# Block attention and FFN on one core: the FFN's first products join the attention's ring of PSUM banks, and the order of a far pair's steps changes

## The chip, the cores and the metric

The kernel runs on one core of a Trainium2 chip. The metric is the device time of one execution in microseconds (us); the time of a version is the median of several runs. The engines are TensorE (matrix products; PE in the profile, its weight loads PEld), VectorE (DVE), ScalarE (ACT), GpSimd (POOL) and SyncE (SP), which issues the DMAs. Products land in PSUM, which has 8 banks of 128 x 512 fp32; VectorE and ScalarE read them from there.

## The reference

Shapes: 8 batches, 8 heads, 576 tokens, head size 64; the FFN takes 4608 tokens of width 512 to 2048 and back.

```python
scores = (1.0 / np.sqrt(D)) * np.matmul(q, k.transpose(0, 1, 3, 2))
mask = block_i >= block_j              # blocks of 64 tokens
scores = np.where(mask, scores, -1000000000.0)
attn = np.exp(scores - np.max(scores, axis=-1, keepdims=True))
attn = attn / (np.sum(attn, axis=-1, keepdims=True) + 1e-09)
x = np.matmul(attn, v).transpose(0, 2, 1, 3).reshape(B * S, H * D)
h = x @ w_in
g = np.where(h >= 1, h, np.where(h <= -1, 0.0, (h + 1) ** 2 / 4.0))
out = g @ w_out
```

## The kernel before, in words

Every fp32 operand is held as a high and a low part, and each product is a sum of products of parts, so TensorE has much to do: 6280 products in all.

The attention works on 32 pairs of heads (4 per batch). A pair's work is cut into 8 steps (`attention_steps`, L663), each ended by a `yield`. From step START = 36 on (the fifth step of pair 4) the main loop at the end puts one step of the FFN behind each attention step: by turns `ffn_in` (L763: 12 products of 512 columns into one bank, `ph`, for 512 tokens and 128 of the 2048 columns) and `ffn_out` (L790: 12 products of 512 columns into the four output banks `po`). 66 FFN steps remain when the attention is over. The scheduler of the tile layer fixes the order on each engine when the program is built; it may move an instruction ahead of others, but not past what it depends on.

Pairs of batches 0 and 1 are "near" (and "plain": probabilities kept whole), those of batches 2 to 7 are "far": `self.far = b >= FAR`, FAR = 2. A pair's attention consists of

- scores: for the two heads j and three groups of query tiles g, `scores(j, g)` (L494), and `scores_last` for the last 64 tokens. TensorE makes the scores (L482, L485), VectorE finds the negated maximum (L505), ScalarE the exponential and its sum (L509), VectorE divides (L491, L492, L515), and a DMA copies the probabilities to a buffer `prr` of the type that TensorE turns (`as_float32r`, L230);
- turnings: `turn(j, g)` (L556) and `turn_last` (L572): TensorE transposes probabilities into a bank `ps_t` (L552), ScalarE writes the high part (L545), VectorE the low part (L547). The corner of the last block, a 128 x 64 piece, has a bank of its own in `turn_last`;
- attn*v: `attn_v_first` (the first 256 queries of both heads in one bank) and `attn_v(0)`, `attn_v(1)` (the other 320), products at L591 into `ps_av`; `add_halves` (L608) has ScalarE copy one half (L613) and VectorE add the other (L614). `xtmp`, where the copy goes, has one buffer;
- for the next pair, q and k turned: `turned_raw(j)` (L397) for each head and `turned_last` (L437) for the last blocks, into `ps_qk`; `parted` (L384) takes them out of the bank in turns of ScalarE and VectorE (L388, L389, L394, L395), `turned_last` with two more reads by VectorE (L446).

Every bank `ps_s`, `ps_t`, `ps_av`, `ps_qk` comes from `work_bank` (L80): before the FFN begins by turns from `ps_o`, the four output banks, and from `ps_w`; later from `ps_w` alone, a ring. A new tile of the ring takes the bank of the oldest one, so TensorE waits until the oldest tile's last reader is done. Before the change the ring `ps_w` has three banks, and `ph` a bank of its own (`ps_h`):

```python
ps_w = ctx.enter_context(tc.tile_pool(name="ps_w", bufs=3, space=bass.MemoryType.PSUM))
ps_h = ctx.enter_context(tc.tile_pool(name="ps_h", bufs=1, space=bass.MemoryType.PSUM))
ps_o = ctx.enter_context(tc.tile_pool(name="ps_o", bufs=NTT, space=bass.MemoryType.PSUM))
```

The last reader of `ph` is the maximum at L783, behind ScalarE's L779 and VectorE's L780.

## Time and profile before

| | us |
|---|---|
| median of 3 runs (lowest, highest) | 1269.29 (1268.47, 1269.56) |
| the profiled execution, its own time | 1269.69 |
| its span, first to last instruction | 1267.9 |
| TensorE busy in the span | 1200.1 |
| VectorE, ScalarE, GpSimd busy | 887.0, 703.2, 394.6 |
| mean granted TensorE clock, share of full | 0.981 |

The busy time of an engine counts overlapping instructions once. A row of the timeline gives the start, the time from start to end, and in brackets how long the engine had been idle and what ended that. Products are pipelined: one starts before the one ahead has ended, so the step from start to start is the price of a product, not its duration. Names of lines (L482) are those of the kernel before unless said otherwise; the change shifts lines below L515, so that L547 stands at L560 in it, L552 at L565, L591 at L608, L770 at L799, L794 at L823, L799 at L828.

### The profile page before, as it was taken

The page shows a single profiled execution, that of the slowest core. Times are in us where ns is not written, and L with a number is a line of the kernel's source. Part 1 is how long each engine was busy: PE and PEld are TensorE (multiplying, and loading weights), DVE is VectorE, ACT ScalarE, POOL GpSimd, SP SyncE. Part 2 cuts the span into 40 slices and gives each one's busy share as a digit, 9 for nine tenths or more (in the row PEclk, how much of TensorE's full clock was granted, in tenths as well). Part 3 has the DMA queues.
Part 4 walks back from the last instruction along what each step waited for, and adds up shares of the span by engine and source line. Part 5 has one row for each costly group of instructions (what it writes and reads, how often), then busy time and mean ns, then how long its engine had stood idle before and what let it go on. Part 6 is the DMA issues. An engine that isn't in the chain of part 4 may idle for free.

```text
span 1267.9 us, 20253 instructions
## 1 busy us (share of the span) xinstructions
PE 1200.1 (95%) x6280; PEld 998.8 (79%) x6280; DVE 887.0 (70%) x2188; ACT 703.2 (55%) x1827; POOL 394.6 (31%) x430
## 2 busy tenths in 40 slices
PE   5888889899999999999999999999999999999998
PEld 4666667678888888888888888888888888888886
DVE  8898877758777777777777777787777777322222
ACT  5787656646566655665656655566556555222222
POOL 3555655522222222222222222222222222222222
PEclk9888988999999999999999999999999999999999
DMA  5566666667888655555554655465556433422432
GB/s 158 167 176 215 203 228 197 217 198 237 260 273 266 215 162 158 154 175 163 156 162 145 187 157 152 138 189 153 160 154 190 137 128 118 132 87 98 133 100 100
DMA packets 185259, 215.43 MB, mean 170 GB/s; under 512 B 113840, under 2 KB 132272, under 8 KB 184384
## 3 DMA queue, kind: packets, MB, share of 16 engines
q1 hardware_dynamic: 185152, 214.14, 54.9%
q8 instruction: 50, 0.82, 0.3%
q14 instruction: 57, 0.47, 0.1%
HBM read 134.74 MB, written 31.98 MB: 131 GB/s over the span
## 4 chain that ended last, share of the span: by engine, by line
PE 69%; DVE 16%; ACT 6%; issue 5%; DMA 1%; POOL 1%; SPq 1%; ACTq 0%; POOLq 0%; DVEq 0%
PE ph L770 29%; PE po L794 15%; PE po L799 7%; PE ps_av L591 7%; PE ps_s L482 4%; ACT pr L509 3%; PE ps_s L485 3%; DVE t L780 2%; PE ps_t L552 2%; DVE t L783 2%; ACT t L779 2%; DVE pb L547 2%; DVE nm L505 2%; DVE sm L491 1%; DVE pr L515 1%
## 5 line engine op out<-in xcount | busy, mean ns | idle before, releaser
L785 POOL TENSOR_TENSOR gl<-t,gh 128x512 fp32r<-128x512 f32 x144 | 187.5, 1302 | 510.2 <-ACT gh L784 333.2
L794 PE MATMUL po<-wo,gh 128*128 128x512 f32 x1152 | 296.1, 397 | 0.5 <-DMA wo<-wo_split 0.3
L794 PEld LDWEIGHTS po<-wo,gh 128*128 128x128 f32 x1152 | 212.5, 189 | 44.5 <-DMA wo<-wo_split 0.7
L770 PE MATMUL ph<-xh,wih 128*128 128x512 f32 x576 | 232.9, 404 | 1.6 <-DVE t L783 1.6
L770 PE MATMUL ph<-xh,wil 128*128 128x512 f32 x576 | 228.8, 397 | 0.0
L770 PE MATMUL ph<-xl,wih 128*128 128x512 f32 x576 | 227.8, 396 | 0.5 <-DVE xl L627 0.5
L780 DVE SCALAR_TENSOR_TENSOR t<-t 128x512 f32<-128x512 f32 x144 | 101.5, 705 | 168.0 <-ACT t L779 165.2
L779 ACT ACTIVATE t<-ph 128x512 f32<-128x512 f32 x144 | 85.9, 597 | 173.8 <-PE ph L770 173.8
L509 ACT ACTIVATE pr<-ps_s,nm 128x128 f32<-128x128 f32 (+3 forms) x256 | 134.1, 527 | 60.5 <-DVE nm L505 58.4
L784 ACT CAST gh<-t 128x512 fp32r<-128x512 f32 x144 | 89.5, 621 | 120.3 <-DVE t L783 120.0
L799 PE MATMUL po<-wo,gl 128*128 128x512 f32 x576 | 155.6, 392 | 0.0
L482 PE MATMUL ps_s<-ka,qa 68*128 68x288 f32 (+4 forms) x384 | 135.3, 367 | 15.0 <-ACT pr L509 5.4
L379 POOL TENSOR_TENSOR vsr<-vn,vsr 128x256 fp32r<-128x256 f32 (+1 forms) x96 | 55.2, 576 | 246.2 <-ACT vsr L378 244.6
L770 PEld LDWEIGHTS ph<-xh,wil 128*128 128x128 f32 x576 | 109.5, 190 | 23.8
L770 PEld LDWEIGHTS ph<-xh,wih 128*128 128x128 f32 x576 | 109.8, 191 | 21.7 <-DVE t L783 2.3
L799 PEld LDWEIGHTS po<-wo,gl 128*128 128x128 f32 x576 | 108.7, 189 | 23.1
L505 DVE TENSOR_REDUCE nm<-ps_s 128x1 f32<-128x128 f32 (+3 forms) x256 | 118.8, 482 | 10.4 <-PE ps_s L485 9.4
L770 PEld LDWEIGHTS ph<-xl,wih 128*128 128x128 f32 x576 | 109.7, 190 | 20.5 <-DVE xl L627 0.9
L485 PE MATMUL ps_s<-kb,qb 128*128 128x288 f32 (+4 forms) x384 | 121.1, 322 | 0.0
L515 DVE TENSOR_SCALAR pr<-pr,sm 128x128 f32<-128x128 f32 (+3 forms) x256 | 107.3, 440 | 5.4
L783 DVE TENSOR_TENSOR t<-ph,t 128x512 f32<-128x512 f32 x144 | 98.7, 686 | 2.2
L491 DVE TENSOR_SCALAR sm<-sm 128x1 f32<-128x1 f32 (+1 forms) x224 | 52.0, 232 | 68.3 <-ACT pr L509 65.7
(111 smaller groups left out, 1871.4 us busy)
## 6 DMA issues: line engine op xcount, KB each, us to landing
wo<-wo_split SPq DMA_DIRECT2D x144, 512.0 KB, 3.5
prr<-pr SPq DMA_DIRECT2D x96, 192.0 KB, 2.5
prr<-pr SPq DMA_DIRECT2D x72, 256.0 KB, 2.8
out_dram<-ob SPq DMA_DIRECT2D x36, 256.0 KB, 2.9
bits<-in_moe_w_in_dram SPq DMA_DIRECT2D x32, 256.0 KB, 3.5
bits<-in_moe_w_out_dram SPq DMA_DIRECT2D x32, 256.0 KB, 3.0
wo_split<-ws SPq DMA_DIRECT2D x16, 512.0 KB, 2.9
qa<-qb SPq DMA_DIRECT2D x63, 128.0 KB, 2.4
```

The source lines that it names most:

```text
L482: nc.tensor.matmul(ps, qa[:KA, j, c0 : c0 + P], ka[:KA, j, k0 : k0 + n], start=first, stop=False)
L485: nc.tensor.matmul(ps, qb[:, j, c0 : c0 + P], kb[:, j, k0 : k0 + n], start=False, stop=last)
L505: nc.vector.tensor_reduce(out=nm[:, i : i + 1], in_=ps[:, cs], axis=AX.X, op=ALU.max, negate=True)
L509: nc.scalar.activation(pr[:, cs], ps[:, cs], AF.Exp, bias=nm[:, i : i + 1], scale=1.0, accum_out=sm[:, i : i + 1],)
L515: nc.vector.tensor_scalar_mul(pr[:, cs], pr[:, cs], sm[:, i : i + 1])
L770: nc.tensor.matmul(ph, w[:, cc, fs], x[:, cc, xs], start=(cc == 0 and i == 0), stop=(cc == NCC - 1 and i == 2),)
L779: nc.scalar.activation(t_, ph, AF.Relu, bias=0.5, scale=0.5)
L780: nc.vector.scalar_tensor_tensor(out=t_, in0=t_, scalar=1.0, in1=t_, op0=ALU.min, op1=ALU.mult)
L783: nc.vector.tensor_tensor(out=t_, in0=ph, in1=t_, op=ALU.max)
L785: nc.gpsimd.tensor_tensor(out=gl, in0=t_, in1=gh.bitcast(F32), op=ALU.subtract)
L794: nc.tensor.matmul(po[tt], gh[:, ts_], wo[:, w, :], start=(fc == 0 and w == 0), stop=False)
L799: nc.tensor.matmul(po[tt], gl[:, ts_], wo[:, 0, :], start=False, stop=fc == NFC - 1)
```

## The change

The pool `ps_h` goes, `ps_w` gets a fourth bank, and `ffn_in` takes its bank from `work_bank`. For far pairs: scores come first in every step, and the copy DMA of the probabilities is issued at the end of the step (`move`); attn*v's three parts stand in steps 1, 2 and 3 of the next pair (they stood in step 8 and in steps 1 and 3); the last block's corner is turned in the bank of `turn(1, 0)`; q and k of the next pair's second head are turned in step 7 and its last blocks in step 8 (they stood in step 8 and in the next pair's step 2). `attn_v_first` takes `xtmp` once for both heads. No product, reduction or DMA is added or taken away.

```diff
-    ps_w = ctx.enter_context(tc.tile_pool(name="ps_w", bufs=3, space=bass.MemoryType.PSUM))
-    ps_h = ctx.enter_context(tc.tile_pool(name="ps_h", bufs=1, space=bass.MemoryType.PSUM))
+    ps_w = ctx.enter_context(tc.tile_pool(name="ps_w", bufs=4, space=bass.MemoryType.PSUM))
...
-            self.pr[j, g] = as_float32r(pr[:, : cols[-1].stop], self.plain) if self.hop else [pr]
+            self.pr[j, g] = [pr[:, : cols[-1].stop]]
+            if not self.far:
+                self.moved(j, g)
+
+        def moved(self, *key):
+            if self.hop:
+                self.pr[key] = as_float32r(self.pr[key][0], self.plain)
+
+        def move(self, *key):
+
+            if self.far:
+                self.moved(*key)
...
             for c0 in range(0, n, P):
                 self.transposed(ps[:, c0 : c0 + P], pr, c0, P)
+            if self.far and j == 1 and g == 0:
+                self.turn_corner(self.pr.pop(("last",)), ps[:BLK, n : n + P])
...
-            ps = work_bank("ps_t")
-            self.transposed(ps[:BLK, :P], pr, SM, BLK)
-            self.split(
-                ps[:BLK, :P].rearrange("p (h c) -> p h c", h=2), *(x[:BLK] for x in self.pc)
-            )
+            if not self.far:
+                self.turn_corner(pr, work_bank("ps_t")[:BLK, :P])
+
+        def turn_corner(self, pr, ps):
+
+            self.transposed(ps, pr, SM, BLK)
+            self.split(ps.rearrange("p (h c) -> p h c", h=2), *(x[:BLK] for x in self.pc))
...
-            if far:
-                old.turn(1, 1)
             if cur:
                 cur.scores(0, 0)
                 cur.turned(False, 1)
                 cur.load("v")
             if far:
-                old.attn_v_first()
+                old.turn(1, 1)
+                old.attn_v(0)
             if near:
                 old.turn(1, 2)
+            if cur:
+                cur.move(0, 0)
             yield
+            if cur:
+                cur.scores(0, 1)
+                if not cur.raw:
+                    cur.turned_last()
...
             if far:
                 old.turn(1, 2)
-            if cur:
-                cur.scores(0, 1)
-                cur.turned_last()
...
+                old.attn_v_first()
...
             if far:
+                if cur:
+                    cur.scores(0, 2)
                 old.attn_v(1)
                 old.store_x()
...
             if cur.far:
                 cur.begin()
+                cur.scores_last()
                 cur.turn(0, 0)
-                cur.scores_last()
...
-            if cur.far:
-                cur.turn(0, 1)
-                cur.scores(1, 0)
-            else:
-                cur.scores(1, 0)
-                cur.turn(0, 2)
+            cur.scores(1, 0)
+            cur.turn(0, 1 if cur.far else 2)
+            cur.move(1, 0)
...
+            cur.scores(1, 1)
             if cur.far:
                 cur.turn(0, 2)
-                cur.scores(1, 1)
...
+            cur.scores(1, 2)
             if cur.far:
                 cur.turn_last()
-                cur.scores(1, 2)
+                if nxt:
+                    nxt.turned(True, 1)
...
             if cur.far:
                 cur.turn(1, 0)
-                cur.attn_v(0)
...
-            if nxt:
+            if nxt and not cur.far:
                 nxt.turned(True, 1)
+            if nxt and nxt.raw:
+                nxt.turned_last()
             yield
...
-        ph = ps_h.tile([P, 512], F32, tag="ph", name="ph")
+        ph = work_bank("ph")
```

How the order on the engines changes is shown at three places. TensorE before, from the FFN's second products behind step 1 of a far pair to the next first products (`ps_qk` by L442 is the next pair's last blocks of q and k, here in step 2):

```order
L794 MATMUL po<-wo,gh 128x512 x8
L799 MATMUL po<-wo,gl 128x512 x4
L552 MATMUL ps_t<-ident_r,prr 128x128 x4
L482 MATMUL ps_s<-ka,qa 128x384
L485 MATMUL ps_s<-kb,qb 128x384
L442 MATMUL ps_qk<-ident_r,qk 128x128
L770 MATMUL ph<-xh,wih 128x512
```

The three ring tiles ahead of L442's are `attn_v_first`'s, the turning's and the scores', so L442 takes the bank of `attn_v_first`.

TensorE now, steps 7 and 8 of a far pair:

```order
L482 MATMUL ps_s<-ka,qa 128x512
L485 MATMUL ps_s<-kb,qb 128x512
L565 MATMUL ps_t<-ident_r,prr 128x128 x4
L401 MATMUL ps_qk<-ident_r,qk 128x128 x4
L823 MATMUL po<-wo,gh 128x512 x8
L828 MATMUL po<-wo,gl 128x512 x4
L565 MATMUL ps_t<-ident_r,prr 128x128 x3
L565 MATMUL ps_t<-ident_r,prr 64x128
L442 MATMUL ps_qk<-ident_r,qk 128x128
L799 MATMUL ph<-xh,wih 128x512
```

The scores stand ahead of the turning, the corner (64x128) behind the three transposes of `turn(1, 0)` in one bank, and L442 behind them. Behind the twelve products of `ph` come `scores(0, 0)`, three transposes and `attn_v(0)`, the fourth ring tile behind L442's.

VectorE now, from the division of `scores(1, 2)` to the last read of that bank:

```order
L515 TENSOR_SCALAR pr<-pr,sm 128x512
L395 TENSOR_TENSOR kb<-ps_qk,kb 64x512
L560 TENSOR_TENSOR pcs_107<-ps_t,pcs_106 64x128
L389 SCALAR_TENSOR_TENSOR qb<-ps_qk,qb 64x2x64
L560 TENSOR_TENSOR pa_6201<-ps_t,pa_6200 128x384
L395 TENSOR_TENSOR kb<-ps_qk,kb 64x2x64
L446 TENSOR_SCALAR qa<-ps_qk 64x2x64
L446 TENSOR_SCALAR ka<-ps_qk 64x2x64
```

Before, only a division and a maximum stood between L389 and the reads at L446; now the pieces of the second head's q and k (64x512), of the corner (`pcs`) and of the turning (`pa`) stand among them.

## Rows read from the trace of the kernel before

**Rows 1.** the page's line on TensorE, whole run

```profile
PE 1200.1 (95%) x6280; PEld 998.8 (79%) x6280; DVE 887.0 (70%) x2188; ACT 703.2 (55%) x1827; POOL 394.6 (31%) x430
```

**Rows 2.** busy time by stretch: us, PE, PEld, DVE, ACT, POOL, PEclk, DMA, GB/s

```profile
200.00:250.00 50.00, 42.34 (x189) 32.76 (x189) 38.21 (x91) 30.83 (x86) 27.81 (x36) 0.90 0.65 212
...
600.00:650.00 50.00, 48.95 (x276) 41.58 (x275) 38.44 (x96) 29.44 (x75) 12.47 (x13) 1.00 0.48 145
```

**Rows 3.** waits of TensorE, 290 to 1070 us: total, times, longest

```profile
PE ps_qk L442 <- DVE x L614: 8.9, 23, 0.4
PE ps_s L482 <- ACT pr L509: 5.2, 17, 0.3
```

**Rows 4.** the tile ps_qk, 290 to 1070 us: duration min/median/max, first and last start

```profile
L442 PE MATMUL ps_qk<-ident_r,qk x23: 249/252/254, 311.8 to 1047.2; 128*128 128x128 f32 x23
...
L446 DVE TENSOR_SCALAR ka<-ps_qk x23: 293/293/294, 315.2 to 1050.6; 64x128 fp32r<-64x128 f32 x23
```

**Rows 5.** timeline of TensorE: start, us, what, [idle before]

```profile
611.83 0.34 PE L485 MATMUL ps_s<-kb,qb 128*128 128x384 f32 x1
612.55 0.25 PE L442 MATMUL ps_qk<-ident_r,qk 128*128 128x128 f32 x1 [0.38 <-DVE x L614]
...
616.72 0.47 PE L482 MATMUL ps_s<-ka,qa 68*128 68x512 f32 x1
...
617.27 2.00 PE L794 MATMUL po<-wo,gh 128*128 128x512 f32 x8
...
631.54 0.51 PE L552 MATMUL ps_t<-ident_r,prr 128*128 128x128 f32 x5
632.35 0.50 PE L482 MATMUL ps_s<-ka,qa 68*128 68x512 f32 x1 [0.30 <-ACT pr L509]
```

**Rows 6.** timeline of VectorE, the same pair

```profile
608.95 0.68 DVE L783 TENSOR_TENSOR t<-ph,t 128x512 f32<-128x512 f32 x1
...
610.08 0.41 DVE L614 TENSOR_TENSOR x<-ps_av,xtmp 64x256 f32<-64x256 f32 x1
...
611.98 0.43 DVE L614 TENSOR_TENSOR x<-ps_av,xtmp 64x256 f32<-64x256 f32 x1
...
631.04 0.55 DVE L505 TENSOR_REDUCE nm<-ps_s 128x1 f32<-128x384 f32 x1
```

**Rows 7.** timeline of ScalarE, the same pair

```profile
607.13 0.60 ACT L779 ACTIVATE t<-ph 128x512 f32<-128x512 f32 x1 [0.74 <-PE ph L770]
...
611.25 0.37 ACT L613 COPY xtmp<-ps_av 64x256 f32<-64x256 f32 x1
...
631.62 0.58 ACT L509 ACTIVATE pr<-ps_s,nm 128x384 f32<-128x384 f32 x1 [2.13 <-DVE nm L505]
```

**Rows 8.** timeline of TensorE in batch 1 and the first pair of batch 2

```profile
239.59 0.39 PE L482 MATMUL ps_s<-ka,qa 68*128 68x512 f32 x1
...
240.05 0.38 PE L552 MATMUL ps_t<-ident_r,vsr 128*128 128x128 f32 x3
240.26 2.08 PE L794 MATMUL po<-wo,gh 128*128 128x512 f32 x8
...
274.23 0.34 PE L485 MATMUL ps_s<-kb,qb 128*128 128x384 f32 x1
274.41 0.22 PE L442 MATMUL ps_qk<-ident_r,qk 128*128 128x128 f32 x1
```

**Rows 9.** VectorE by shape, 290 to 1070 us: busy, mean ns, idle before

```profile
L395 DVE TENSOR_TENSOR kb<-ps_qk,kb 64x512 fp32r<-64x512 f32 x46 | 31.9, 693 | 15.6 <-ACT kb L394 14.9
...
L547 DVE TENSOR_TENSOR pa<-ps_t,pa 128x384 fp32r<-128x384 f32 x46 | 25.5, 555 | 20.6 <-ACT pa L545 20.6
...
L547 DVE TENSOR_TENSOR pcs<-ps_t,pcs 64x128 fp32r<-64x128 f32 x24 | 6.6, 274 | 0.0
```

**Rows 10.** timeline of TensorE in batch 0

```profile
88.86 0.46 PE L770 MATMUL ph<-xh,wih 128*128 128x512 f32 x1
```

**Rows 11.** waits of TensorE, whole run

```profile
PE ph L770 <- DVE t L783: 1.6, 3, 0.7
```

More of the change, by code (lines that the diff above doesn't have):

```diff
@@ L541, in scores_last @@
             nc.vector.tensor_scalar_mul(pr, pr, sm[:, 2:3])
-            self.pr["last"] = as_float32r(pr, self.plain) if self.hop else [pr]
+            self.pr["last",] = [pr]
+            if not self.far:
+                self.moved("last")
         def split(self, ps, hi, lo=None):
@@ L572, in turn_last @@
         def turn_last(self):
-            pr = self.pr.pop("last")
+            pr = self.pr["last",] if self.far else self.pr.pop(("last",))
             ps = work_bank("ps_t")
@@ L580, in turn_last @@
             )
-            ps = work_bank("ps_t")
-            self.transposed(ps[:BLK, :P], pr, SM, BLK)
-            self.split(
-                ps[:BLK, :P].rearrange("p (h c) -> p h c", h=2), *(x[:BLK] for x in self.pc)
-            )
+            if not self.far:
+                self.turn_corner(pr, work_bank("ps_t")[:BLK, :P])
+        def turn_corner(self, pr, ps):
+            self.transposed(ps, pr, SM, BLK)
+            self.split(ps.rearrange("p (h c) -> p h c", h=2), *(x[:BLK] for x in self.pc))
         def weighted(self, ps, j, parts, first=True, last=True):
@@ L606, in parts, with add_halves @@
             return (*parts, (NTL, SM - G0, [x[:, j, :] for x in self.pc]))
-        def add_halves(self, ps, j, c0):
+        def add_halves(self, ps, j, c0, xtmp):
             main = slice(j * D, (j + 1) * D)
@@ L611, in add_halves @@
             n = ps.shape[1]
-            xtmp = att1.tile([P, G1], F32, tag="xtmp", name="xtmp")
             nc.scalar.copy(xtmp[main, :n], ps[rest, :])
@@ L636, in attn_v_first @@
                 self.weighted(ps[:, j * G0 : (j + 1) * G0], j, self.parts_first(j))
+            xtmp = att1.tile([P, G1], F32, tag="xtmp", name="xtmp")
             for j in range(2):
-                self.add_halves(ps[:, j * G0 : (j + 1) * G0], j, 0)
+                self.add_halves(ps[:, j * G0 : (j + 1) * G0], j, 0, xtmp)
         def attn_v(self, j):
@@ L644, in attn_v @@
             self.weighted(ps, j, self.parts(j))
-            self.add_halves(ps, j, G0)
+            self.add_halves(ps, j, G0, att1.tile([P, G1], F32, tag="xtmp", name="xtmp"))
         def store_x(self):
@@ L698, in attention_steps @@
                 old.store_x()
+            if cur:
+                cur.move(0, 1)
             yield
             if far:
+                if cur:
+                    cur.scores(0, 2)
                 old.attn_v(1)
                 old.store_x()
-            if not cur:
-                return
-            if cur.far:
+                if not cur:
+                    return
+                if not cur.far:
+                    cur.begin()
+                    cur.turn(0, 0)
+            elif cur.far:
                 cur.scores(0, 2)
@@ L710, in attention_steps @@
                 cur.turn(0, 0)
+            cur.move(0, 2)
             yield
@@ L718, in attention_steps @@
                 cur.turn(0, 1)
+            cur.move("last")
             if nxt:
@@ L724, in attention_steps @@
                 nxt.split_k()
-            if cur.far:
-                cur.turn(0, 1)
-                cur.scores(1, 0)
-            else:
-                cur.scores(1, 0)
-                cur.turn(0, 2)
+            cur.scores(1, 0)
+            cur.turn(0, 1 if cur.far else 2)
+            cur.move(1, 0)
             if nxt:
@@ L733, in attention_steps @@
             yield
+            cur.scores(1, 1)
             if cur.far:
                 cur.turn(0, 2)
-                cur.scores(1, 1)
             else:
-                cur.scores(1, 1)
                 cur.turn_last()
+            cur.move(1, 1)
             if nxt:
@@ L742, in attention_steps @@
             yield
+            cur.scores(1, 2)
             if cur.far:
                 cur.turn_last()
-                cur.scores(1, 2)
+                if nxt:
+                    nxt.turned(True, 1)
             else:
-                cur.scores(1, 2)
                 cur.attn_v(0)
                 cur.turn(1, 0)
+            cur.move(1, 2)
             yield
```

4 lines of the change are left out of this document (2 added, 2 removed).

## The prediction

> **What bounds the kernel now.** I read the page's first lines, then busy time by stretch, then who waited for whom, then the timelines of one pair. TensorE is busy for 1200.1 us of a span of 1267.9 [rows 1], and nothing else comes near, so what counts is the time in which TensorE stands still while it has work. There are two regimes [rows 2]. In batch 1 (about 115 to 280 us; the row from 200 to 250 stands for it) TensorE is busy for 42.34 us of 50, at a mean granted clock of 0.90: here it waits for the other engines. From about 290 to 1070 us, where the far pairs run, it is busy for 48.95 us of 50 at a clock of 1.00. The tail has FFN alone, and the change touches nothing there.
>
> In the far stretch TensorE's waits have two entries only [rows 3]: L442 (the last blocks of q and k) waits 23 times, 8.9 us in all, for VectorE's add L614, and the scores' L482 waits 17 times, 5.2 us in all, for ScalarE's exponential L509. The first and last start of L442 in this stretch are 311.8 and 1047.2, with 23 of them [rows 4], so a pair takes (1047.2 - 311.8) / 22 = 33.43 us.
>
> The idle times understate the loss, because pipelined products overlap; I price a stall from start to start. First stall: L485's 384 columns start at 611.83 and L442 at 612.55 [rows 5], 0.72 us; undisturbed, a 384-column product takes 274.41 - 274.23 = 0.18 [rows 8]. The loss is **0.54 us**. Second stall: five transposes start at 631.54 and the scores behind them at 632.35 [rows 5], 0.81 us; a transpose takes (240.26 - 240.05) / 3 = 0.07 [rows 8], five take 0.36. The loss is **0.45 us**. Together 0.99 us per pair.
>
> Both are ring waits. In the first, L442 needs `attn_v_first`'s bank, three tiles back; VectorE's second add to it starts only at 611.98, behind the first add at 610.08 [rows 6] and ScalarE's second copy at 611.25 [rows 7]. In the second, `scores(1, 2)` needs the bank of `scores(1, 1)`, three tiles back because the corner takes a tile of its own; its maximum starts at 631.04 [rows 6] and its exponential at 631.62 [rows 7].
>
> **The change part by part.**
>
> *The two stalls go.* In the changed order L442 takes the bank of `scores(1, 2)`, four tiles back, with a whole `ffn_out` between them, and `scores(1, 2)` that of the first head's q and k, with an `ffn_in` and an `ffn_out` between. `attn_v_first`'s bank goes to the first bank of `scores_last`, five products' worth of attention and two FFN steps later. Gain 0.99 us per pair.
>
> *`ph` in the ring.* From ScalarE's start on `ph` at 607.13 [rows 7] to the end of the maximum, 608.95 + 0.68 [rows 6], is 2.5 us. Each `ph` bank is asked for again four tiles later, past three attention tiles and one `ffn_out` of some 2.7 us (the twelve products of `ffn_out` end where the next step begins). The cover is that FFN step; were it gone, about 1 us would show. I cost it at nothing.
>
> *Scores first.* A 512-column pair of score products behind `attn_v(1)` takes 617.27 - 616.72 = 0.55 [rows 5], behind the FFN's products 240.05 - 239.59 = 0.46 [rows 8]: weights are loaded under a long product, not under a short one. Six of the score groups now lose a short predecessor; four FFN steps gain one. Two net, at 0.09, is 0.18 us per pair gained. Bounds: nothing, and 0.5 if the FFN steps pay nothing.
>
> *The new wait.* `attn_v(0)`, now in step 1 of the next pair, takes the bank of L442, now in step 8. Between their starts TensorE has the twelve products of `ph`, `scores(0, 0)` and three transposes: about 2.8 + 0.5 + 0.2 = 3.5 us. In the kernel before, that bank is free after the last L446: 1050.6 + 0.29 - 1047.2 = 3.7 us after L442's start [rows 4]. So 0.2 us would be lost per pair at that speed. Above that bound: 64x512 L395, `pcs` and `pa` stand ahead of, or among, the bank's reads on VectorE, at 0.69, 0.27 and 0.55 us [rows 9]; if none of them overlaps the wait there was before, 1.5 us more. Below: the five reads of the bank by themselves, nothing lost. The row of the same chain is nearest, since VectorE had a `pb` split, a maximum and a division among those reads before as well: I take **0.2 us**, and keep 0 to 1.7.
>
> What stands behind `attn_v(0)` on TensorE is the next `ffn_out`; nothing else waits for it in less than a step.
>
> The corner shares the bank of `turn(1, 0)` now. The nearest rows are those of `attn_v_first`, two halves in one bank: copy, add, copy and add take turns there, with the second copy at 611.25 behind the first add's end at 610.49 [rows 6, 7], though the one buffer of `xtmp` asks for that as well. If the two splits of this bank take turns too, ScalarE stands still for the 0.27 us of `pcs` [rows 9] and a hand-over each way, and the chain of the new wait is that much longer (a rival, below). [...]
>
> *The DMAs.* The copies of probabilities are issued at the end of a step, one or two products later than before, but behind the division that they wait for in any case, about 3 us after the scores; turnings follow three steps later, over 10 us. On SP's queue they are passed by the q and k copies of `turned_raw`, whose data is done earlier. Nothing, and the cover is wide. The value loads move behind one more copy and are wanted two pairs later.
>
> *The early part.* `ph` had a bank of its own, so the scheduler put the first twelve products of the FFN into gaps of batch 0, three at a time, as at 88.86 [rows 10]. In a ring they stay in place, and TensorE does them in batch 1: twelve at 0.23 us (half of the 512-column pair in [rows 8]) is 2.8 us, at most twice that at half the clock. Against it, TensorE waited 1.6 us in all for L783 before it could reuse `ph` [rows 11], which the ring takes away. TensorE is not the limit all the time there, so I take +1 us, bounds -4 and +6: the order in this stretch changes at many places, and its waits belong to other engines.
>
> **The sum.** Per far pair -0.99 - 0.18 + 0.2 = -0.97 us, for the 23 pairs with a far predecessor -22.3; early part +1. From the profiled execution's 1269.7 that gives 1248.4. Its time lies 0.4 above the median shown, so I state **1248**, 1.7% below the median.
>
> **The rivals.**
>
> *Half of it is given back.* Both stalls go, but the bank's splits take turns and the new wait is 0.2 + 0.27 and a hand-over or two of about 0.05 each, so 0.5 to 0.6 us, for which I put 0.55. Then a pair gains 0.62 us: 1269.7 - 14.3 + 1 - 0.4 = 1256. For it: the chain of the bank's reads has several hand-overs between ScalarE and VectorE, and more stands among them now. Against it: part of that work is over before L442 is done, as the corner is turned ahead of it.
>
> *Slower.* At the same place, the wait of `attn_v(0)` for L446: all 1.5 us of the bound are paid, plus the 0.2, and more where VectorE comes late to the chain from `scores(1, 2)`. It decides at 0.99 + 0.18 = 1.17 us of waiting per pair. At 1.7 us the loss is 0.53 per pair: 1269.7 + 12.2 + 1 - 0.4 = 1282. Against it: VectorE's work per pair does not grow, and it is busy for 38.44 us of 50 [rows 2], so it can catch up.
>
> *The early part eats it.* Without FFN products to fill gaps, batch 1 could lose the 6 us of the bound in place of 1: 1253 with the rest as forecast.
>
> *The change does not do what it says* for the stalls: if the waits only move on (each ring tile is released as late as before, and the fourth bank is used up by `ph`), the time is within 0.2% of 1269, about what a measurement of this kernel can tell from no change. Against it: between L442 and its new donor lies a whole FFN step.
>
> **How the numbers follow.** Forecast, both stalls gone, 0 to 0.4 us of new wait, the early part within its bounds: 1240 to 1253, chance 0.60. Half given back: 1254 to 1259, chance 0.20. No change: 0.05. Slower: 0.08. The remaining 0.07 is a gain above the forecast. So faster by over 0.2%: 0.87; within: 0.05; slower: 0.08. The range takes in the forecast and the half: 1240 to 1260.
>
> **What would show it.** Right: TensorE's waits in the far stretch have neither L442 for L614 nor L482 for L509; a pair takes about 32.5 us between starts of L442; `attn_v(0)`'s first product starts within 0.3 us of the transposes' end. Wrong: a wait of `ps_av` for L446 of over 0.5 us per pair, a wait of `ph`'s first product for an attention bank, or a far stretch that begins some microseconds later than at 280 us, where it begins now.

## The result, and the profile after

The changed kernel takes 1272.88 us (median of 9 runs, 1270.28 to 1273.69) against 1268.47 for the kernel before (9 runs, 1264.14 to 1269.56): the ratio is **1.0033**, 95% interval 1.0023 to 1.0043. It is slower by 0.3%, where 1248 was forecast. The span went from 1267.9 to 1271.3 us in the two profiled executions. The page's busy times and its chain of waits, by engine, after:

```profile
PE 1195.4 (94%) x6280; PEld 1004.6 (79%) x6280; DVE 933.3 (73%) x2188; ACT 704.1 (55%) x1827; POOL 395.4 (31%) x430
...
PE 58%; DVE 28%; ACT 6%; issue 3%; DMA 3%; POOL 1%; SPq 1%; ACTq 0%; POOLq 0%; DVEq 0%
```

Against [rows 1] one engine stands out. VectorE executes the same 2188 instructions and is busy 46.3 us longer; it now has 28% of the chain that ended last (16% before). The waits of TensorE from 290 to 1070 us (total, times, longest), as in [rows 3], without two entries that occur once each:

```profile
PE ps_av L608 <- DVE ka L446: 12.1, 22, 0.6
PE ps_t L565 <- DVE pb L560: 1.9, 5, 0.4
```

Both waits of [rows 3] are gone, as forecast, and the one that was feared is there in 22 pairs. Its place on TensorE, where L442 is the last blocks of q and k, L565 is `turn(1, 1)` and L608 is `attn_v(0)`:

```profile
638.58 0.24 PE L442 MATMUL ps_qk<-ident_r,qk 128*128 128x128 f32 x1
...
641.84 0.28 PE L485 MATMUL ps_s<-kb,qb 128*128 128x256 f32 x1
642.25 0.42 PE L565 MATMUL ps_t<-ident_r,prr 128*128 128x128 f32 x3
643.22 1.32 PE L608 MATMUL ps_av<-pb,vsr 128*128 128x320 f32 x8 [0.55 <-DVE ka L446]
```

From start to start this costs more than the 0.55 us of idle time. The turning comes 0.41 us behind the scores and `attn_v(0)` 0.97 us behind the turning; where nothing waits (the run with the division later, below) these are 0.12 and 0.24. So the price is 0.29 + 0.73 = **1.0 us** per pair, all that the two stalls of before had cost. The turning waits too, for the bank of `turn(1, 0)`, four tiles back, whose last reader is the split `pa`. VectorE in the same pair, from the reciprocal of `scores(1, 2)` to the last read of L442's bank, and GpSimd:

```profile
638.45 0.17 DVE L492 RECIPROCAL sm<-sm 128x1 f32<-128x1 f32 x1
638.65 1.36 DVE L515 TENSOR_SCALAR pr<-pr,sm 128x512 f32<-128x512 f32 x1
640.03 0.69 DVE L395 TENSOR_TENSOR kb<-ps_qk,kb 64x512 fp32r<-64x512 f32 x1
...
641.59 0.56 DVE L560 TENSOR_TENSOR pa<-ps_t,pa 128x384 fp32r<-128x384 f32 x1 [0.23 <-ACT pa L558]
...
642.78 0.29 DVE L446 TENSOR_SCALAR ka<-ps_qk 64x128 fp32r<-64x128 f32 x1
```

```profile
638.42 1.30 POOL L814 TENSOR_TENSOR gl<-t,gh 128x512 fp32r<-128x512 f32 x1 [6.85 <-ACT gh L813]
```

The division L515 at 128x512 takes 1.36 us here. It starts while GpSimd's subtraction `gl` (the FFN's low part) runs, and ends 0.29 us after `gl` does, at 640.01 against 639.72: of its time, 0.87 us are waiting (1.36 - 0.49). The other work of the chain takes what it took before ([rows 9] for L395, `pcs` and `pa`). The same division over 330 to 1030 us (busy, mean ns, idle before), with the addition of 1e-9 to the sums, L491, which stands ahead of a reciprocal; first now, then before:

```profile
L515 DVE TENSOR_SCALAR pr<-pr,sm 128x512 f32<-128x512 f32 x42 | 35.4, 843 | 1.4
L491 DVE TENSOR_SCALAR sm<-sm 128x2 f32<-128x2 f32 x42 | 24.7, 587 | 15.5 <-ACT pr L509 14.9
```

```profile
L515 DVE TENSOR_SCALAR pr<-pr,sm 128x512 f32<-128x512 f32 x42 | 20.8, 494 | 1.5
L491 DVE TENSOR_SCALAR sm<-sm 128x2 f32<-128x2 f32 x42 | 21.0, 500 | 20.5 <-ACT pr L509 20.5
```

The division of a 128x384 tile is longer too, at a mean of 651 ns where it was 420, but that is not `gl`: half of these divisions take 0.88 us, under another subtraction of GpSimd, `vsr` (L379, a low part of v), as at 616.50 with `vsr` from 616.43 to 617.17. Without `gl` their mean is 655.

Where the 3.4 us of span went: I take the first product of `scores_last` in each far pair (24 of them, 23 periods). It starts at 287.78 in the first pair and at 1058.13 in the last; before, at 286.20 and 1054.82. So 1.6 us were lost ahead of the far stretch and 1.7 in it. Three pairs of four take 33.32 to 33.38 us (33.45 to 33.51 before); every fourth, in which `ffn_out` also copies its output rows (two copies on VectorE), takes 33.90 to 33.96 (33.22 to 33.31 before). There VectorE is late at one more place, the second row of the waits above.

### The profile page after: what moved, and what is told of

It reads as the page before. It is cut to its first block, busy times and chain, and to the rows that moved or that the text cites. A ratio compares the mean times of both kernels' runs of the same rounds, so it can differ in the third digit from the quotient of the medians.

```text
span 1271.3 us, 20237 instructions
## 1 busy us (share of the span) xinstructions
PE 1195.4 (94%) x6280; PEld 1004.6 (79%) x6280; DVE 933.3 (73%) x2188; ACT 704.1 (55%) x1827; POOL 395.4 (31%) x430
## 4 chain that ended last, share of the span: by engine, by line
PE 58%; DVE 28%; ACT 6%; issue 3%; DMA 3%; POOL 1%; SPq 1%; ACTq 0%; POOLq 0%; DVEq 0%
PE ph L799 20%; PE po L823 14%; PE ps_av L608 8%; PE po L828 7%; DVE pr L515 4%; DVE nm L505 3%; DVE kb L395 3%; PE ps_s L482 3%; PE ps_s L485 2%; DVE pb L560 2%; DVE t L809 2%; DVE t L812 2%; DVE qb L389 2%; PE ps_t L565 2%; DVE sm L491 1%
## 5 line engine op out<-in xcount | busy, mean ns | idle before, releaser
L814 POOL TENSOR_TENSOR gl<-t,gh 128x512 fp32r<-128x512 f32 x144 | 192.8, 1339 | 609.7 <-ACT gh L813 419.0
L823 PEld LDWEIGHTS po<-wo,gh 128*128 128x128 f32 x1152 | 208.1, 188 | 40.9 <-DMA wo<-wo_split 1.5
L799 PE MATMUL ph<-xh,wih 128*128 128x512 f32 x576 | 236.7, 411 | 3.6 <-ACT pb L558 2.3
L509 ACT ACTIVATE pr<-ps_s,nm 128x128 f32<-128x128 f32 (+3 forms) x256 | 134.1, 527 | 62.9 <-DVE nm L505 62.3
L505 DVE TENSOR_REDUCE nm<-ps_s 128x1 f32<-128x128 f32 (+3 forms) x256 | 123.5, 485 | 31.6 <-PE ps_s L485 28.5
L515 DVE TENSOR_SCALAR pr<-pr,sm 128x128 f32<-128x128 f32 (+3 forms) x256 | 132.6, 538 | 4.9
L482 PE MATMUL ps_s<-ka,qa 68*128 68x288 f32 (+4 forms) x384 | 122.5, 333 | 8.8 <-ACT kb L427 2.5
L379 POOL TENSOR_TENSOR vsr<-vn,vsr 128x256 fp32r<-128x256 f32 (+1 forms) x96 | 50.7, 528 | 152.0 <-ACT vsr L378 150.5
L558 ACT CAST pb<-ps_t 128x512 fp32r<-128x512 f32 (+1 forms) x120 | 65.4, 545 | 46.7 <-PE ps_t L565 44.3
```

What stands on the lines that cost most here:

```text
L482: nc.tensor.matmul(ps, qa[:KA, j, c0 : c0 + P], ka[:KA, j, k0 : k0 + n], start=first, stop=False)
L505: nc.vector.tensor_reduce(out=nm[:, i : i + 1], in_=ps[:, cs], axis=AX.X, op=ALU.max, negate=True)
L509: nc.scalar.activation(pr[:, cs], ps[:, cs], AF.Exp, bias=nm[:, i : i + 1], scale=1.0, accum_out=sm[:, i : i + 1],)
L515: nc.vector.tensor_scalar_mul(pr[:, cs], pr[:, cs], sm[:, i : i + 1])
L799: nc.tensor.matmul(ph, w[:, cc, fs], x[:, cc, xs], start=(cc == 0 and i == 0), stop=(cc == NCC - 1 and i == 2),)
L814: nc.gpsimd.tensor_tensor(out=gl, in0=t_, in1=gh.bitcast(F32), op=ALU.subtract)
```

## The experiments

Theory A: the gain is used up by the wait of `attn_v(0)`, because the new order puts VectorE's division under `gl`, and while `gl` runs that division can't. Rivals: the ring of four costs something itself; the chain on VectorE is too long in any case; VectorE has become the bound. Each run was timed beside the kernel before, which took 1267.1 to 1268.0 us there (1268.5 beside the changed kernel). "Far" is the stretch of 23 periods, "pair" the common period and that of each fourth pair:

| run | median, us | ratio to before, 95% | far, us | pair, us |
|---|---|---|---|---|
| before | | | 768.6 | 33.47; 33.23 |
| changed | 1272.9 | 1.0023 to 1.0043 | 770.4 | 33.35; 33.90 |
| new order, old banks | 1269.5 | 1.0007 to 1.0037 | 770.5 | 33.35; 33.95 |
| old order, ring of four | 1267.6 | 0.9989 to 1.0020 | 766.7 | 33.37; 33.10 |
| `gl` in halves | 1266.8 | 0.9984 to 1.0010 | 765.6 | 32.95; 34.23 |
| L442 in step 2 | 1264.2 | 0.9965 to 0.9993 | 763.9 | 33.02; 33.60 |
| L442 in step 1 | 1265.4 | 0.9969 to 0.9997 | 764.4 | 33.06; 33.65 |
| division on ScalarE | 1260.5 | 0.9930 to 0.9962 | 759.2 | 32.72; 33.77 |
| L442 in step 1, division on ScalarE | 1266.1 | 0.9977 to 0.9997 | 765.3 | 33.06; 33.65 |
| changed, no `gl` | 1244.0 | 0.9793 to 0.9835 | 750.3 | 32.45; 33.11 |
| division later | 1252.9 | 0.9862 to 0.9900 | 753.4 | 32.41; 33.46 |
| before, no `gl` | 1245.7 | 0.9805 to 0.9843 | 752.2 | 32.65; 32.85 |
| before, no addition | 1268.7 | 0.9997 to 1.0026 | 764.0 | 33.15; 33.35 |
| `gl` on VectorE | 1254.6 | 0.9883 to 0.9929 | 760.8 | 32.92; 33.30 |

### The two halves of the change apart

New order, old banks:

```diff
-    ps_w = ctx.enter_context(tc.tile_pool(name="ps_w", bufs=4, space=bass.MemoryType.PSUM))
+    ps_w = ctx.enter_context(tc.tile_pool(name="ps_w", bufs=3, space=bass.MemoryType.PSUM))
+    ps_h = ctx.enter_context(tc.tile_pool(name="ps_h", bufs=1, space=bass.MemoryType.PSUM))
...
-        ph = work_bank("ph")
+        ph = ps_h.tile([P, 512], F32, tag="ph", name="ph")
```

> The new order with the old banks: ring of three, the FFN's first products in a bank of their own. Theory A (the wait that takes the gain back is that of attn_v(0) for the bank of L442, because VectorE's division L515 of scores(1, 2) is stretched to 1.35 us while GpSimd's subtraction gl runs): the bank of attn_v(0) is still that of L442, now three tiles back, so the wait stays at about 1 us per pair, a far pair takes 33.4 us as with the whole change, and only the early part returns (1.5 us): 1270 to 1272. Rival (the ring of four itself costs, because the FFN's first products are now in it): a pair gets back to 32.5 us, about 1250.

The old order with the ring of four is the same edit the other way, made in the kernel before.

> The old order with the ring of four. Theory A (the order decides, the ring alone moves the first stall on): the wait of L442 for attn_v_first's bank goes to the first products of ph, one tile later, which take that bank now, at 0.4 to 0.5 us; scores(1, 2) still take the bank of scores(1, 1), or the corner's, and wait up to 0.45: 1268 to 1271. Rival (the fourth bank by itself removes the first stall, 0.54 us in 23 pairs): 1256 to 1258.

Waits of TensorE in the far stretch, new order with old banks, then old order with the ring:

```profile
PE ps_av L609 <- DVE ka L447: 12.6, 23, 0.6
```

```profile
PE ph L769 <- DVE x L613: 8.2, 23, 0.6
PE ps_s L481 <- ACT pr L508: 6.1, 17, 0.6
```

Both layouts hold eight banks of 128 x 512 (3 + 1 + 4 and 4 + 4). The new order alone has the new wait, at 12.6 us against 12.1, and the same far stretch to 0.1 us: the slower pairs come from the order, not from the ring. The ring alone moves L442's stall on by one tile, to the first products of `ph`, and keeps the other: within 0.2% of before. Both came out as theory A had it, each some half a microsecond below its range.

### `gl` in two instructions

```diff
-        nc.gpsimd.tensor_tensor(out=gl, in0=t_, in1=gh.bitcast(F32), op=ALU.subtract)
+        for h in (slice(0, TCH // 2), slice(TCH // 2, TCH)):
+            nc.gpsimd.tensor_tensor(
+                out=gl[:, h], in0=t_[:, h], in1=gh[:, h].bitcast(F32), op=ALU.subtract
+            )
```

> The changed kernel with GpSimd's subtraction gl in two instructions of 256 columns in place of one of 512. Theory A (VectorE is shut out for as long as one GpSimd instruction runs): L515 at 128x512 falls from a mean of 0.84 us towards 0.6 and in the pair from 1.35 to 0.9 to 1.0, the wait of attn_v(0) shrinks by about 0.4 us per pair, 8 to 10 us in all: 1262 to 1265. Rival (the chain on VectorE is simply too long, gl does not matter): no change, 1272 to 1274, or longer by the fixed cost of 256 more instructions on GpSimd.

The direction was right, the size half (the edit adds 144 instructions, not the 256 that the rival names). VectorE and GpSimd in a common pair (from 601.17), and, in the same two views, in a fourth pair (from 567.57):

```profile
568.26 1.02 DVE L515 TENSOR_SCALAR pr<-pr,sm 128x512 f32<-128x512 f32 x1
...
601.39 0.80 DVE L515 TENSOR_SCALAR pr<-pr,sm 128x512 f32<-128x512 f32 x1
```

```profile
567.57 1.43 POOL L815 TENSOR_TENSOR gl<-t,gh 128x256 fp32r<-128x256 f32 x2 [7.43 <-ACT gh L813]
...
601.17 1.62 POOL L815 TENSOR_TENSOR gl<-t,gh 128x256 fp32r<-128x256 f32 x2 [6.85 <-PE po L831]
```

In the common pair the division takes 0.80 us in place of 1.36 and ends 0.60 us ahead of the second half, so I read it as standing between the halves. The halves take 1.62 us, where they take 1.43 in the fourth pair and the one instruction 1.30: now GpSimd is held up, by 0.19 us. The pair gains 0.40 us. In the fourth pair the division arrives as the first half ends and sits out the second, which ends at 569.00, 0.28 before it: 1.02 us, where the changed kernel has 0.87 in such a pair. These pairs lose 0.3. The addition L491 of two columns got longer as well, 0.70 us at 559.46 and 0.75 at 575.50 where the changed kernel has a mean of 0.59.

### Moving L442 instead

In step 2, as before the change:

```diff
-                if not cur.raw:
-                    cur.turned_last()
+                cur.turned_last()
...
-            if nxt and nxt.raw:
-                nxt.turned_last()
```

> The changed kernel with L442 (the last blocks of q and k) back in the pair's own step 2, behind scores(0, 1); everything else as changed. Theory A (the wait is the one of attn_v(0) for L442's bank): attn_v(0) now takes the bank of turn(1, 0) or an older one, which is free in time; the wait of L608 for L446 is gone and a pair takes 32.4 to 32.7 us: 1250 to 1259. Rival (VectorE has become the bound, since it is busy 46 us longer; a wait that is removed comes back elsewhere): 1270 to 1275.

In step 1, behind `attn_v(0)`:

```diff
                 old.attn_v(0)
+            if far and cur and cur.raw:
+                cur.turned_last()
...
-            if nxt and nxt.raw:
+            if nxt and nxt.raw and not cur.far:
                 nxt.turned_last()
```

> The changed kernel with L442 (the last blocks of q and k) issued in step 1 of the pair itself, behind attn_v(0). Behind this stands what the run with L442 in step 2 showed: the wait for L446 went, but the first products of ph behind step 2 then asked for the bank of scores(0, 1) four tiles back and started 0.67 us late in each pair. Theory A (each ring wait is decided by which tile stands four back): now ph's donor is L442's bank, with a whole FFN step between, attn_v(0)'s is turn(1, 0)'s and scores(0, 1)'s is scores(0, 0)'s; the pair takes 32.4 to 32.6 us (33.5 with the change, 33.2 with L442 in step 2): 1248 to 1254. Rival (VectorE is the bound, at some 28 us of 33 per pair, and a wait removed at one place returns at another): 1262 to 1268.

With the division on ScalarE as well:

> Both edits: L442 in step 1 behind attn_v(0), and the division of scores(1, 2) on ScalarE. Theory A: no ring wait is left that is decided by VectorE; a pair takes 32.3 to 32.5 us: 1247 to 1252, up to 3 us below the run with L442 in step 1 alone. Rival (once the waits are gone the division on ScalarE delays other copies there): equal to or above the run with L442 in step 1 alone.

Each time the wait for L446 was gone and another tile of the ring had one. With L442 in step 2 (1264.2 us, above theory A's 1250 to 1259 and below the rival's 1270), on TensorE:

```profile
610.77 0.50 PE L796 MATMUL ph<-xh,wih 128*128 128x512 f32 x1 [0.31 <-ACT pr L509]
```

With L442 in step 1, who held up TensorE's weight loads:

```profile
PEld ps_qk L442 <- DVE t L814: 5.4, 23, 0.4
```

Here four tiles ahead of L442 is a `ph`, whose last reader L814 comes late. I had looked at the donors of `ph`, `attn_v(0)` and the scores, but not at L442's own, so 1265.4 came in place of 1248 to 1254; the rival's sentence that a wait removed returns elsewhere fits these three runs, though its reason, an amount of work that VectorE can't do, does not fit the last one below. The row does not account for all of the 0.65 us by which such a pair is longer than one of the best version below (33.06 against 32.41); where the rest goes is not shown. Moving the division to ScalarE on top of it brought nothing (1266.1 us where theory A gave 1247 to 1252, and the same common period, 33.06), as the rival had it; nothing waited for L446 any more.

### Taking the division out of the chain

On ScalarE, for `scores(1, 2)` of far pairs:

```diff
-                nc.vector.tensor_scalar_mul(pr[:, cs], pr[:, cs], sm[:, i : i + 1])
+                if self.far and (j, g) == (1, 2):
+                    nc.scalar.activation(pr[:, cs], pr[:, cs], AF.Copy, scale=sm[:, i : i + 1])
+                else:
+                    nc.vector.tensor_scalar_mul(pr[:, cs], pr[:, cs], sm[:, i : i + 1])
```

> The changed kernel with the division L515 of scores(1, 2) of far pairs done by ScalarE in place of VectorE; all else as changed. Theory A (the wait of attn_v(0) is long because this one instruction stands on VectorE for 1.35 us, shut out by GpSimd's gl): VectorE's chain to L446 is 1.35 us shorter, ScalarE's some 0.7 us longer; the wait of 1 us per pair falls under 0.3 and a pair takes 32.5 to 32.9 us: 1252 to 1259. Rival (the chain from L395 to L446 with its turns of ScalarE and VectorE is itself too long): at most 0.2 us per pair, 1266 to 1271.

11 us faster than the changed kernel (by the ratios, 1.0033 - 0.9946), 1.5 us above theory A's range. What is left is in ScalarE's and VectorE's queues:

```profile
599.84 0.72 ACT L516 ACTIVATE pr<-pr,sm 128x512 f32<-128x512 f32 x1
600.59 0.26 ACT L561 CAST pcs<-ps_t 64x128 fp32r<-64x128 f32 x1
```

```profile
600.88 0.28 DVE L563 TENSOR_TENSOR pcs<-ps_t,pcs 64x128 fp32r<-64x128 f32 x1 [0.34 <-ACT pcs L561]
```

The division stands ahead of ScalarE's copy of `pcs`, and VectorE waits 0.34 us for that.

On VectorE, but behind L446. The scheduler put a division that was merely written later in the same place as ever, so a small instruction (zero times an element of `ka`, added to the sums) ties it to L446:

```diff
+            if cur.far:
+                if nxt and nxt.raw:
+                    total = cur.left[1][:BLK, 0:1]
+                    nc.vector.scalar_tensor_tensor(
+                        out=total, in0=ka[:BLK, 0, SM : SM + 1].bitcast(F32), scalar=0.0,
+                        in1=total, op0=ALU.mult, op1=ALU.add,
+                    )
+                cur.divide()
+                cur.move(1, 2)
             yield
             old = cur
```

> The changed kernel with the division L515 of scores(1, 2) of far pairs still on VectorE, but behind the two reads L446: a small VectorE instruction adds zero times an element of ka, which L446 writes, to the sums, so the scheduler can't place the division ahead. Theory A (the division is shut out by gl only because of where it stands; behind L446 gl is over): the division takes 0.49 us, L446 ends about 1.3 us earlier, attn_v(0) waits under 0.15 us, and a pair takes 32.4 to 32.6 us, near the 32.45 of the run without gl, some more in each fourth pair: 1245 to 1252. Rival (the division comes under another GpSimd instruction, or delays the next maximum or the turning of (1, 2)): 1255 to 1262, no better than the run with the division on ScalarE (1260.5).

VectorE and TensorE in a common pair (L524 is the division, L614 `attn_v(0)`; `gl` runs from 596.00 to 597.29):

```profile
599.39 0.29 DVE L446 TENSOR_SCALAR ka<-ps_qk 64x128 fp32r<-64x128 f32 x1
...
599.91 0.48 DVE L524 TENSOR_SCALAR pr<-pr,sm 128x512 f32<-128x512 f32 x1
```

```profile
599.47 0.28 PE L485 MATMUL ps_s<-kb,qb 128*128 128x256 f32 x1
599.59 0.37 PE L571 MATMUL ps_t<-ident_r,prr 128*128 128x128 f32 x3
599.83 1.31 PE L614 MATMUL ps_av<-pb,vsr 128*128 128x320 f32 x8
```

The division takes 0.48 us and `attn_v(0)` does not wait. A common pair takes 32.41 us, 0.94 less than with the change. At 1252.89 us (1.2% below the kernel before, interval 0.9862 to 0.9900) it has the lowest median of the versions that compute everything (the run with `gl` on VectorE is close, and the two intervals overlap), 0.9 us above the range given: I had not allowed enough for the fourth pairs, which still take 33.46. TensorE still waits there at two places, for VectorE each time: `turn_last` (L571) for a split `pb` (5 times, 1.8 us in all) and `attn_v(0)` for L446 (6 times, 2.3 us in all).

### Without `gl`, in both kernels

The same edit in both; the second products read `gh` where they read `gl`:

```diff
-        nc.gpsimd.tensor_tensor(out=gl, in0=t_, in1=gh.bitcast(F32), op=ALU.subtract)
...
-        return gh, gl, wo
+        return gh, gh, wo
```

> The changed kernel without GpSimd's subtraction gl; the second products of the FFN read gh in place of gl, so the part gl of the products is left out and the count of products stays. Theory A (gl shuts VectorE out): L515 at 128x512 returns to 0.49 us, L491 at 128x2 to under 0.2, the wait of L608 for L446 shrinks to 0.1 to 0.3 us per pair: 1250 to 1256. Rival (something else on VectorE or in SBUF stretches L515, such as the copy DMAs): L515 stays near 0.84 and the time at 1268 to 1272.

> The kernel before without GpSimd's subtraction gl, its second products of the FFN reading gh in its place, as in the run of the changed kernel without gl (1244.0; the part gl of the products is left out). Theory A (gl costs much only where the new order puts L515 under it; in the kernel before the same L515 starts when gl has just ended): only small gains, L491 at 128x2 from 0.50 to 0.17: 1262 to 1268. Rival (gl costs some 27 us in either kernel, by holding up the second products or VectorE at large, and the change only inherits that): 1240 to 1246.

Changed kernel without `gl`, VectorE, then TensorE:

```profile
587.53 0.49 DVE L515 TENSOR_SCALAR pr<-pr,sm 128x512 f32<-128x512 f32 x1
...
590.79 0.29 DVE L446 TENSOR_SCALAR ka<-ps_qk 64x128 fp32r<-64x128 f32 x1
```

```profile
590.95 0.37 PE L565 MATMUL ps_t<-ident_r,prr 128*128 128x128 f32 x3
591.23 1.32 PE L608 MATMUL ps_av<-pb,vsr 128*128 128x320 f32 x8
```

From the start of the division to the end of L446 it is 3.55 us in place of 4.42; the difference of 0.87 is that of the division alone (1.36 - 0.49). `attn_v(0)` starts 0.28 us behind the turning, 0.04 later than where nothing waits. Theory A holds for the changed kernel, and the time of 1244.0 is 6 us below its range. Of the gain, 20.0 us lie in the far stretch; the far stretch also starts 9.9 us earlier in the profiled execution (277.88 against 287.78), and what `gl` holds up ahead of it was not traced.

For the kernel before my expectation was wrong, and the rival's range holds: it gains 22 us without `gl`, nearly as much (16.4 in the far stretch, which starts 7.9 us earlier). Kernel before without `gl`, at the places of the two old stalls of [rows 5] and on VectorE ahead of them:

```profile
584.06 0.51 PE L552 MATMUL ps_t<-ident_r,prr 128*128 128x128 f32 x5
584.45 0.50 PE L482 MATMUL ps_s<-ka,qa 68*128 68x512 f32 x1
...
597.46 0.34 PE L485 MATMUL ps_s<-kb,qb 128*128 128x384 f32 x1
597.85 0.25 PE L442 MATMUL ps_qk<-ident_r,qk 128*128 128x128 f32 x1
```

```profile
596.88 0.17 DVE L491 TENSOR_SCALAR sm<-sm 128x2 f32<-128x2 f32 x1 [0.76 <-ACT pr L509]
...
613.44 0.17 DVE L491 TENSOR_SCALAR sm<-sm 128x2 f32<-128x2 f32 x1 [0.27 <-ACT pr L509]
```

Scores follow the five transposes after 0.39 us (0.81 before), L442 the scores after 0.39 (0.72 before). The same instruction in the kernel before with `gl`, and GpSimd there:

```profile
611.26 0.48 DVE L491 TENSOR_SCALAR sm<-sm 128x2 f32<-128x2 f32 x1 [0.78 <-ACT pr L509]
...
628.30 0.59 DVE L491 TENSOR_SCALAR sm<-sm 128x2 f32<-128x2 f32 x1 [0.27 <-ACT pr L509]
```

```profile
610.43 1.29 POOL L785 TENSOR_TENSOR gl<-t,gh 128x512 fp32r<-128x512 f32 x1 [0.98 <-ACT gh L784]
...
627.58 1.29 POOL L785 TENSOR_TENSOR gl<-t,gh 128x512 fp32r<-128x512 f32 x1 [5.84 <-issue]
```

An addition of two columns takes 0.48 and 0.59 us and ends with `gl` both times (611.74 against 611.72, 628.89 against 628.87). Behind it on VectorE's queue stand the add L614 of [rows 6], for which L442 waited, and the maximum at 631.04 for which L509 and then the scores waited. So most of the two stalls that the change removed was the doing of `gl` as well (0.33 of 0.54 us, and 0.42 of 0.45); L614 and L509 only carried the delay on.

To test that by the small instruction alone, the kernel before without the addition:

```diff
-            nc.vector.tensor_scalar_add(total, total, EPS)
```

> The kernel before without VectorE's addition L491 of 1e-9 to the sums (a sum is at least 1, so the addition does not change it in fp32). What stands behind it: without gl both old stalls were gone, and in the kernel before L491 at 128x2 takes 0.48 and 0.59 us there, in place of 0.17, and ends with gl. Theory A (the two old stalls too come from gl, by way of this one small instruction): for L442 the reciprocal and the add L614 start at once, under gl, and its stall of 0.54 us shrinks to 0.2 or less; behind scores(0, 0) and at the other head the next instruction is a division, which gl shuts out in the same way, so the second stall of 0.45 us stays: 0.35 to 0.5 us per pair, 1256 to 1260. Rival (L491 is only 0.17 us of work, and its long time is harmless): at most 0.17 us per pair, 1263 to 1267.

VectorE (L514 is the divisions of `scores(0, 0)`, L613 the add), then TensorE, at the places of the two old stalls:

```profile
614.29 0.61 DVE L514 TENSOR_SCALAR pr<-pr,sm 128x128 f32<-128x128 f32 x2
614.92 0.43 DVE L613 TENSOR_TENSOR x<-ps_av,xtmp 64x256 f32<-64x256 f32 x1
```

```profile
614.66 0.34 PE L485 MATMUL ps_s<-kb,qb 128*128 128x384 f32 x1
615.50 0.25 PE L442 MATMUL ps_qk<-ident_r,qk 128*128 128x128 f32 x1 [0.50 <-DVE x L613]
...
634.49 0.51 PE L551 MATMUL ps_t<-ident_r,prr 128*128 128x128 f32 x5
634.83 0.50 PE L482 MATMUL ps_s<-ka,qa 68*128 68x512 f32 x1
```

It came out the other way round than I expected. The stall ahead of the scores is gone (0.34 us behind the transposes). That ahead of L442 grew from 0.72 to 0.84, because the scheduler now puts the two divisions, 0.61 us, ahead of the add. The common pair gains 0.32 us and the far stretch 4.6, but in the profiled execution the stretch begins at 290.6 us in place of 286.2, and the median stays. So the run shows that the second stall came by way of the addition. For the first it shows only what the new order costs, and the gain I stated did not come.

### `gl` on VectorE

```diff
-        nc.gpsimd.tensor_tensor(out=gl, in0=t_, in1=gh.bitcast(F32), op=ALU.subtract)
+        nc.vector.tensor_tensor(out=gl, in0=t_, in1=gh.bitcast(F32), op=ALU.subtract)
```

> The changed kernel with the subtraction gl on VectorE in place of GpSimd: nothing runs on GpSimd beside most of VectorE's chains, but VectorE gets 144 instructions of about 0.68 us more, 98 us in all, 2.7 us in a pair. Theory A (the price of gl is the exclusion, not the work): L515 at 128x512 returns to 0.49 us, L491 at 128x2 to 0.17, and although VectorE has more to do the time falls well below the changed kernel's 1271: 1248 to 1260. Rival (VectorE is the bound, its sheer amount of work decides): 1272 to 1300.

VectorE by shape from 330 to 1030 us (busy, mean ns, idle before):

```profile
L814 DVE TENSOR_TENSOR gl<-t,gh 128x512 fp32r<-128x512 f32 x85 | 60.5, 711 | 0.0
...
L515 DVE TENSOR_SCALAR pr<-pr,sm 128x512 f32<-128x512 f32 x43 | 20.8, 484 | 0.8
...
L491 DVE TENSOR_SCALAR sm<-sm 128x2 f32<-128x2 f32 x42 | 7.1, 170 | 2.4
```

VectorE has 144 instructions more, and is busy for 965.8 us in place of 933.3; the kernel is 16 us faster than the changed one (by the ratios, 1.0033 - 0.9906), within theory A's range. VectorE's amount of work is not what made the changed kernel slow: where its instructions stood against GpSimd's was. The added work is not free all the same. The wait for L446 is still there (22 times, 7.8 us in all), since `gl` now stands ahead of the division in the same chain, and a common pair takes 32.92 us where it takes 32.45 without `gl`.

## Why the prediction was wrong

- **The two stalls go:** right. Neither is left, and the new order without `gl` shows no wait in a common pair, at 32.45 us; "about 32.5 us" stood in the prediction.
- **The new wait, 0.2 us:** this is the step that failed. The place, the donor bank and the chain were the ones named; the size was 1.0 us. The bank was taken to be free 3.7 us after L442's start, as in the kernel before, on the ground that VectorE had a split, a maximum and a division among the bank's reads there too. In the trace of that kernel the split and the maximum stand ahead of the first of these reads, L389 at 614.21; between it and L446 are L491, L492, a division of 0.42 us and the read L395, no maximum, and none of them under GpSimd. In the pair shown above the bank is free after 642.78 + 0.29 - 638.58 = 4.5 us. The division of `scores(1, 2)`, now at the head of the chain, had no term of its own, and none allowed for GpSimd: in the new place it starts under `gl` and takes 1.36 us in place of 0.49. Without `gl` `attn_v(0)` starts 0.04 us late, so the pieces that the bound counted, up to 1.5 us, cost nothing, and the rest of this term's working was sound. The turning's own wait of 0.29 us, at the same chain, had been left out. The far stretch missed its forecast by 24.0 us (1.7 lost, 22.3 forecast as a gain); 0.8 us in each of 23 pairs make 18.4 of them.
- **"VectorE's work per pair does not grow":** right of the list of instructions, wrong of the time that VectorE needs for it. From 290 to 1050 us, now and before (columns as in [rows 2]; VectorE's is the third busy time):

```profile
290.00:1050.00 760.00, 742.75 (x4129) 635.83 (x4129) 629.39 (x1445) 457.33 (x1178) 201.48 (x210) 1.00 0.59 177
```

```profile
290.00:1050.00 760.00, 745.88 (x4141) 631.97 (x4139) 589.21 (x1446) 458.21 (x1180) 201.42 (x211) 1.00 0.58 177
```

  Of the 40.2 us more, 38.8 are in four groups that come under GpSimd's subtractions: the divisions at 128x512 (15.9) and 128x384 (9.8), the minimum L544 (8.9) and L491 at 128x2 (4.2). What grew is waiting that the profile counts as busy. This sentence was the argument against the rival that ended slower.
- **The rivals.** "Slower" had the place, and in "more where VectorE comes late to the chain" a word of the cause; its 1.5 us of L395, `pcs` and `pa` were not what was paid, since they stand in the chain without `gl` too. With 1.0 us the common pairs still gain 0.12 us each, and the fourth pairs, which no case treated by themselves, give it back with 0.67 us each. "Half of it is given back" had the splits of one bank take turns: in the pair shown they do (ScalarE's `pa` starts at 641.07, 0.03 us behind the end of VectorE's `pcs`, and VectorE's `pa` at 641.59, 0.04 behind the end of ScalarE's, [0.23 <-ACT pa L558]; what makes them is not shown), but the run without `gl` pays for it and has no wait, so it is not what cost the gain.
- **`ph` in the ring, nothing:** right for the far stretch; 770.4 us with the ring and 770.5 without.
- **Scores first, -0.18:** not shown. Without `gl` the common pairs of the two orders differ by 0.20 us, of which L442's remaining delay in the old order (0.39 - 0.18 = 0.21) is all. What the term was read from is in the trace of before: behind `attn_v(1)` the weights of L482 are loaded from 616.69, 0.03 us ahead of the product, behind the FFN's product from 239.36, 0.23 ahead.
- **The early part, +1:** 1.6 us in one execution each, within its bounds. The half clock of the upper bound occurs in the kernel before: 0.50 from 180 to 185 us, where the first products of the FFN at 179.67 and 180.10 are 0.43 us apart in place of 0.23. The start of the far stretch lies between 281 and 291 us in the kernels with `gl` on GpSimd, one execution each, and at 278 to 280 in the three where GpSimd does not run it; what part of that each edit of the order has there was not tried.

What stays open: why VectorE is late in the fourth pairs of the best version (its two copies of output rows are there, but no run moved them), what `gl` costs ahead of the far stretch, and whether a kernel with the division later and the old bank for `ph` would be faster still.

## What to carry to other kernels

A duration from a row holds for the place in which the instruction stood (the division of 128x512: 0.49 us, and 1.36 under `gl`). Before moving VectorE's work, look at what GpSimd does in the new place, and look at the kernel as it is for small VectorE instructions with two durations (in this one 0.17 and 0.5 us for 128x2): the stalls that the waits put down to an add or an exponential further on began at one. And where a stall goes with a new ring, follow each tile to the one whose bank it takes, the moved one included: three of the edits here only changed which tile waits.

## What the runs showed of the hardware

While GpSimd subtracts (two operands in SBUF), some VectorE instructions hardly advance, and others are untouched. Held up by `gl`: the division of a 128x512 tile in SBUF by a column (0.49 to 1.36 us, ending 0.29 us after `gl`, so that some 0.2 us of its 0.49 passed under it), and the addition of a constant to two columns (0.17 to 0.59 us, ending with `gl`). GpSimd's other subtractions do the same: the division of a 128x384 tile takes 0.88 us under `vsr` in place of 0.42, and the minimum of two single columns, L544, 0.61 under `xl` (L674, the low part of x) in place of 0.16 (624.77 in the changed kernel, with `xl` from 623.94 to 625.36). Not held up: the addition of the same constant to one column (0.15 us at 603.09 in the kernel before, with `gl` from 602.20 to 603.49), the reciprocal (0.17 us at 638.45, with `gl` from 638.42), and the subtraction L395 with one operand in PSUM (0.69 us at 599.85 in the run with the division on ScalarE, with `gl` from 599.21 to 600.50). And where the division comes first, it is `gl` that takes longer: in the changed kernel the division starts at 622.07 and takes 0.49 us, and `gl`, from 622.15, takes 1.56 in place of 1.30 (the halves of `gl` above are another case). That `gl` is what lengthens the division and the addition does not hang on GpSimd's times alone: in the changed kernel without `gl` they take a mean of 487 and 169 ns, where they take 843 and 587 with it. The instructions named as held up have all their operands in SBUF, and the subtraction with one in PSUM was not held up; but the addition to one column and the reciprocal, in SBUF as well, were not either. What decides which is held up the runs do not show. What I had not expected is the size of the effect in a kernel whose GpSimd is busy for 31% of the span: leaving `gl` out is worth 22 us in the one order (ratio 0.9824) and 28 in the other (0.9814 against 1.0033), and giving it to the busier engine still gains 16.
